# Reordering the start of a tuned convolution and SiLU kernel: a block's taps ahead of the next blocks' transposes, the first output matmuls a pair sooner, three warm matmuls out

## Chip, cores, metric

The kernel runs on one core of one Trainium2 chip. The metric is device time in microseconds (us). TensorE is called PE here, its weight loads PEld, VectorE DVE, ScalarE ACT, GpSimd POOL, as in the profile.

## The reference

```python
def _attn_ref(x, weight):              # x (8, 4096, 192), weight (8 heads, 7 taps)
    w = softmax(weight, axis=-1)       # written out in the original
    # causal convolution of 7 taps, one set of taps per head of 24 channels
    out = np.einsum('hk,bskhg->bshg', w, x_unf)
    return out.reshape(B, S, D)
def _moe_ref(x, w_in, w_out, beta):    # w_in (192, 2048), w_out (2048, 192)
    h = x @ w_in
    g = h * (1.0 / (1.0 + np.exp(-beta * h)))
    return g @ w_out                   # on 32768 tokens
```

## The kernel before

Tokens are cut in two halves that occupy the two halves of the array's rows. Per half the work goes in chunks: three small ones first (128, 128 and 256 tokens, called chunk 0, 1 and 2), four of 256, then chunks of 512. For each chunk the hidden matmuls (`mm1`) give `ph` in PSUM, ACT applies SiLU and gives `g`, and the output matmuls (`mm2`) use `g`. Chunks 0 to 2 do `mm1` in eight **pairs** (two hidden chunks of 128 at once).

In steady state the convolution runs on DVE. For the first 512 tokens (**blocks 0 to 3** of 128) there is no time for that, so PE does it with diagonal matrices (`conv_0`, seven taps), after transposing the block. Blocks 4 and 5 are transposed on PE as well, in pair 6 of chunk 1, and then copied by DVE into `xt`, where DVE's own convolution starts. I call this copy **the late blocks' copy**.

```python
    warm(9, 256)                                   # dummy matmuls; their results are not used
    ...
    pin(nc.tensor.matmul(tap_ps, sel..., taps, start=True, stop=True))
    warm(3, 128)                                   # taken out by the change
    ...                                            # softmax of the taps, diagonals
    t = transpose_0(pa[0], x0, 0)                  # block 0
    take_0(t, 0, act=True)
    warm(7, 128)
    ...
    conv_0(b0, 0)                                  # block 0 by seven taps on PE
    ...
    def first_tile(i, u):                          # what follows pair u of chunk i on PE
        if (i, u) == (0, 1):
            take_0(transpose_0(pa[0], xb0, 0), 2)  # block 2: transposes, copy by DVE
            conv_0(pb, 1, 0, 1)                    # block 1: tap 0
        elif (i, u) == (0, 2):
            take_0(transpose_0(pa[1], xb0, 1), 3)  # block 3
            conv_0(pb, 1, 1, 2)
        elif (i, u) == (0, 3):
            conv_0(pb, 1, 2, 5)
        elif (i, u) == (0, 4):
            conv_0(pb, 1, 5, K)
            ...                                    # DVE: evacuate block 1, scale w_out 0 to 3
        ...                                        # blocks 2 and 3 by taps, w_out 4 to 15
        elif (i, u) == (1, 6):
            new_xt(1)
            ts_ = [transpose_0(pb[b], xb1, b) for b in range(2)]     # blocks 4 and 5
            for b in range(2):
                pin(nc.vector.tensor_copy(xt_of[1][...], ts_[b]))    # the late blocks' copy
    ...
    # which output matmuls (of 16 hidden chunks) follow which pair
    for key, us, cuts in (((0, 0), [(1, 4), (1, 5), (1, 6), (1, 7)], (0, 4, 8, 12, 16)), ...
```

`pin` keeps instructions in program order. `w_in` is loaded by POOL's DMA queue in three slices of columns; pair 5 of chunk 0 is the first that needs the third slice (columns 640 on). `w_out` is scaled by 1/beta on DVE (`scale_w_out`) before an output matmul can use it, and later cut into thirds by twelve DVE copies (`part_w_out`).

Of the kernel before, what the change touches and what calls it, by code (L numbers as in the profile page):

```python
# [19 lines left out]
def kernel(  # L20
# [25 lines left out]
    def pin(ins):  # L46

        return tc.keep_in_program_order(ins)
# [27 lines left out]
    def load_x(j, s, b0=0, b1=NB, eng=None):  # L76
        if j not in xf_of:
            xf_of[j] = xf_pool.tile([128, NB, NS, D], FP32, name="xf")
        src = xs[s, TILE * j + 128 * b0:TILE * j + 128 * b1, :]
        pin((eng or nc.sync).dma_start(out=xf_of[j][:, b0:b1, s, :],  # L80
                                       in_=src.rearrange("(b p) d -> p b d", p=128)))

    def cast_x(j, s, b0=0, b1=NB, eng=None):
        if j not in xbf_of:
            xbf_of[j] = xbf_pool.tile([128, NB, NK, NS, Q], BF16, name="xb")
        pin((eng or nc.vector).tensor_copy(  # L86
            xbf_of[j][:, b0:b1, :, s, :].rearrange("p b k q -> p k b q"),
            xf_of[j][:, b0:b1, s, :].rearrange("p b (q k) -> p k b q", k=NK)))

    def new_xt(j):  # L90
        xt_of[j] = xt_pool.tile([128, NK, LEAD + TILE], BF16, name="xt")

    def transpose_x(j, b):
        if j not in xt_of:
            new_xt(j)
        c = LEAD + 128 * b
        pin(nc.sync.dma_start_transpose(
            out=xt_of[j][:, :, c:c + 128],
            in_=xbf_of[j][:, b, :, :, :].rearrange("p k s q -> p (k s q)")))
# [9 lines left out]
    def half_of(s):  # L109
        return slice(64 * s, 64 * s + 64)  # L110
# [62 lines left out]
    def po_banks():  # L173
        return [po_bank(), po_bank()]
# [7 lines left out]
    def warm(n, cols):  # L182
        for _ in range(n):
            pin(nc.tensor.matmul(idle[:, 0, 0:cols], ones[:, 0:128], ones[:, 0:cols], start=True, stop=True))
# [3 lines left out]
    nmax = consts.tile([128, 1], FP32, name="nmax")  # L188
    tap_ps = cv0[:, 1, 0:K]
    pin(nc.tensor.matmul(tap_ps, sel.rearrange("h s g j -> h (s g j)"), taps, start=True, stop=True))  # L190
    warm(3, 128)
    pin(nc.vector.tensor_reduce(out=nmax, in_=tap_ps, axis=AX.X, op=ALU.max, negate=True))
    etap = consts.tile([128, K], FP32, name="etap")
    tsum = consts.tile([128, 1], FP32, name="tsum")
# [14 lines left out]
    def transpose_0(bank, src, b):  # L209

        bf = src.dtype == BF16
        t = (bank.bitcast(BF16) if bf else bank)[:, 0:NK * 128].rearrange("p (k t) -> p k t", k=NK)
        v = src[:, b, :, :].rearrange("p s d -> p (s d)").rearrange("p (m k) -> p k m", k=NK)
        for kk in range(NK):
            pin(nc.tensor.transpose(t[:, kk, :], v[:, kk, :], ident_b if bf else ident))  # L215
        return t

    def take_0(t, b, act=False):
        dst = xr[:, :, PAD + 128 * b:PAD + 128 * b + 128]
        if act:  # L220
            pin(nc.scalar.activation(dst, t, AF.Copy))
        else:
            pin(nc.vector.tensor_copy(dst, t))

    def conv_0(cv, b, k0=0, k1=K):

        for k in range(k0, k1):
            for s in range(NS):
                pin(nc.tensor.matmul(  # L229
                    cv[s][:, 0:NK * 128], diag[half_of(s), k, :, :].rearrange("p s q -> p (s q)"),  # L230
                    xr[half_of(s), :, 128 * b + k:128 * b + k + 128], start=(k == 0), stop=(k == K - 1)))

    def evac_0(cv, b, s, eng):
        i, c = place[b]
        src = cv[s][:, 0:NK * 128].rearrange("p (k t) -> p k t", k=NK)
        dst = xc_of[i][:, s, :, c:c + 128]
        if eng is nc.scalar:
            pin(nc.scalar.activation(dst, src, AF.Copy, scale=rsum))
        else:
            pin(eng.tensor_scalar_mul(dst, src, rsum))  # L240
# [3 lines left out]
    pb = po_banks()  # L244
# [26 lines left out]
    def scale_w_out(c):  # L271
        pin(nc.vector.tensor_scalar_mul(w_out_s[:, c, :], w_out_f[:, c, :], rbeta[:, c:c + 1]))
# [219 lines left out]

    def first_tile(i, u):
        if (i, u) == (0, 1):
            take_0(transpose_0(pa[0], xb0, 0), 2)
            conv_0(pb, 1, 0, 1)
        elif (i, u) == (0, 2):
            take_0(transpose_0(pa[1], xb0, 1), 3)
            conv_0(pb, 1, 1, 2)
        elif (i, u) == (0, 3):  # L500
            conv_0(pb, 1, 2, 5)
        elif (i, u) == (0, 4):
            conv_0(pb, 1, 5, K)
            for s in range(NS):
                evac_0(pb, 1, s, nc.vector)
            for c in range(4):
                scale_w_out(c)
        elif (i, u) == (0, 5):
            conv_0(pa, 2, 0, 2)
        elif (i, u) == (0, 6):  # L510
            conv_0(pa, 2, 2, 5)
        elif (i, u) == (0, 7):
            conv_0(pa, 2, 5, K)
            for s in range(NS):
                evac_0(pa, 2, s, nc.vector)
            for c in range(4, 8):
                scale_w_out(c)
        elif (i, u) == (1, 0):
            conv_0(pb, 3, 0, 2)
        elif (i, u) == (1, 1):  # L520
            conv_0(pb, 3, 2, 5)
        elif (i, u) == (1, 2):
            conv_0(pb, 3, 5, K)
            for s in range(NS):
                evac_0(pb, 3, s, nc.vector)
            for c in range(8, NF):
                scale_w_out(c)
        elif (i, u) == (1, 6):
            new_xt(1)
            ts_ = [transpose_0(pb[b], xb1, b) for b in range(2)]  # L530
            for b in range(2):
                pin(nc.vector.tensor_copy(xt_of[1][:, :, LEAD + 128 * b:LEAD + 128 * b + 128], ts_[b]))
            pin(nc.vector.tensor_copy(xt_of[0][:, :, TILE + LEAD - PAD:],
                                      xr[:, :, TILE:].bitcast(FP32)))
        elif (i, u) == (1, 7):
            for s in range(NS):
                cast_x(1, s, 2, NB)
            for b in range(2, NB):
                transpose_x(1, b)
            for j in (2, 3):  # L540
                for s in range(NS):
                    load_x(j, s)
# [2 lines left out]

    prs_0 = ((0, 0), (1, 0))
    first_mm2 = {}
    for key, us, cuts in (((0, 0), [(1, 4), (1, 5), (1, 6), (1, 7)], (0, 4, 8, 12, 16)),
                          ((1, 0), [(2, 1), (2, 2)], (0, 8, 16)),
                          ((0, 1), [(2, 3), (2, 4)], (0, 8, 16)),  # L550
                          ((1, 1), [(2, 5), (2, 6), (2, 7)], (0, 5, 10, 16))):
        for (i, u), c0, c1 in zip(us, cuts, cuts[1:]):
            first_mm2[(i, u) + key] = range(c0, c1)

    for i in range(n_steps):
        plan = mm2_plan(i - 1) if NP <= i <= NQ else [[] for _ in range(NF)]
        new_g(i, 0)
        if i < NP:
            new_g(i, 1)
        if i < NP:  # L560
            for u in range(NF // 2):
                mm1_pair(i, u)
                first_tile(i, u)
                for ph in (0, 1):
                    for j in range(i):
                        for fc in first_mm2.get((i, u, j, ph), ()):
                            mm2(j, prs_0, ph, fc)
                if i == 2:
                    vector_work(i, 1300, flush=u == NF // 2 - 1)
            continue  # L570
        for u in range(NF):
            if u == NF // 2:
                new_g(i, 1)
            mm1(i, u)
            for t in plan[u]:
                mm2(i - 1, *t)
                if t[1] == 1 and t[2] == NF - 1:
                    budget -= 2 * (D + 60) / 0.96
            if i > NQ:
                mm2_quarters(NM)  # L580
            vector_work(i, 1307 * steps[i][1] // TILE, flush=u == NF - 1)
# [30 lines left out]
```

## Time and profile before

| | before |
|---|---|
| time, first three runs | 687.03 us (687.0 to 687.11) |
| full PE clock from | 5.16 us |
| first activation of pair 0, pair 2, pair 5 of chunk 0 | 8.01, 10.35, 12.95 us |
| first activation of chunk 2 | 21.92 us |
| start of the late blocks' copy on DVE | 20.05 us |
| start of activation 400 (of 576, counted from 0) | 442.88 us |

Times are from the span's start. "Full PE clock from" is the start of the trace's first record of the full clock. Until then PE goes at about half the pace, which I call half clock: a tap of both halves takes 0.32 us and not 0.17, as shown below. The PEclk column of the profile does not show this (it reads 1.00 from 4 us on in before_again, where the first record comes at 9.39). "Activation 400" lies deep in the steady state; it is a good measure of the lead that the start has gained or lost, since the change leaves what follows as it is.

The page of before: span, busy time, and the chain that ended last by engine.

```profile
span 685.2 us, 26902 instructions
...
PE 679.8 (99%) x12368; PEld 501.6 (73%) x12368; DVE 553.0 (81%) x905; ACT 584.0 (85%) x584; POOL 14.6 (2%) x26
...
PE 97%; ACT 1%; DMA 1%; POOL 0%; issue 0%; DVE 0%; POOLq 0%
```

The PE timeline of before around pairs 1 to 5 (start, length, line and operands, count, idle time before it and what ended it):

```profile
7.47 0.83 PE L319 MATMUL ph<-xcp,w_in_s 64*128 64x256 bf16 x12
9.24 0.35 PE L215 MATMUL po<-ident_b,xb 128*128 128x128 bf16 x3 [0.94 <-DMA xb<-in_x_dram]
9.52 0.44 PE L229 MATMUL po<-xr,diag 64*128 64x384 f32 x2
9.80 0.50 PE L319 MATMUL ph<-xcp,w_in_s 64*128 64x256 bf16 x6
10.24 0.35 PE L215 MATMUL po<-ident_b,xb 128*128 128x128 bf16 x3
...
12.38 0.50 PE L319 MATMUL ph<-xcp,w_in_s 64*128 64x256 bf16 x6
```

After pairs 0 and 1 PE stands 0.94 us until block 2 has come in, although the taps of block 1 (L229), whose data DVE had ready at 8.02, stood right behind. ACT waits with it (timeline of ACT, before):

```profile
8.01 1.57 ACT L323 ACTIVATE gp<-ph,beta 128x256 bf16<-128x256 f32 x4 [0.76 <-DVE xr L223]
10.35 0.84 ACT L323 ACTIVATE gp<-ph,beta 128x256 bf16<-128x256 f32 x2 [0.77 <-PE ph L319]
11.35 2.08 ACT L323 ACTIVATE gp<-ph,beta 128x256 bf16<-128x256 f32 x5 [0.16 <-PE ph L319]
```

```profile
20.00:90.00 70.00, 69.68 (x1297) 60.71 (x1295) 69.22 (x123) 68.89 (x100) 0.00 (x0) 1.00 0.48 128
```

### The profile page before, as it was taken

The numbers are of one execution on the slowest core, as the hardware profiler recorded it, in microseconds if no ns is written. First come the engines' busy times: TensorE is split into PE (matmuls) and PEld (weight loads), VectorE is DVE, ScalarE is ACT, GpSimd is POOL, SyncE is SP. The second block draws the span as 40 slices with busy tenths as digits, with TensorE's granted clock in tenths as the row PEclk, the third lists the DMA queues.
The fourth block names the chain that finished last, engine by engine and source line by source line (L and its number), as shares of the span: only waits on it lengthen the run. The fifth ranks groups of instructions, "written<-read, shape, count | busy, mean of one in ns | idle before, by whom it ended". The sixth has DMA issues, their size and how long they took to land.

```text
span 685.2 us, 26902 instructions
## 1 busy us (share of the span) xinstructions
PE 679.8 (99%) x12368; PEld 501.6 (73%) x12368; DVE 553.0 (81%) x905; ACT 584.0 (85%) x584; POOL 14.6 (2%) x26
## 2 busy tenths in 40 slices
PE   8999999999999999999999999999999999999998
PEld 6799767777777777777777777777777777777777
DVE  5999999999988889878889888889888889875112
ACT  7999998888888888888888888888888888888881
POOL 8000000000000000000000000000000000000000
PEclk9999999999999999999999999999999999999999
DMA  9654334344423344423444323344323443220213
GB/s 210 173 163 118 94 94 112 78 118 117 117 57 86 100 112 117 113 56 87 104 112 117 102 63 90 101 117 118 89 58 101 106 117 72 65 52 5 49 48 93
DMA packets 149873, 66.82 MB, mean 98 GB/s; under 512 B 112593, under 2 KB 149153, under 8 KB 149761
## 3 DMA queue, kind: packets, MB, share of 16 engines
q1 hardware_dynamic: 146448, 61.08, 35.4%
q0 software_dynamic: 3168, 3.93, 2.7%
q8 instruction: 96, 1.57, 0.9%
q14 instruction: 17, 0.13, 0.1%
q10 hardware_dynamic: 144, 0.10, 0.1%
HBM read 28.32 MB, written 25.17 MB: 78 GB/s over the span
## 4 chain that ended last, share of the span: by engine, by line
PE 97%; ACT 1%; DMA 1%; POOL 0%; issue 0%; DVE 0%; POOLq 0%
PE ph L336 47%; PE po L414 42%; PE po L368 4%; PE po L452 2%; PE ph L319 1%; ACT gp L323 1%; DMA xb<-in_x_dram 1%; ACT g L323 1%; POOL w_in_s L113 0%; PE po L229 0%; PE po L215 0%; POOL sel L146 0%; DVE o_sp L374 0%; POOL ident L148 0%; POOLq L146 0%
## 5 line engine op out<-in xcount | busy, mean ns | idle before, releaser
L340 ACT ACTIVATE g<-ph,beta 128x1024 bf16<-128x1024 f32 (+1 forms) x528 | 557.7, 1063 | 81.4 <-PE ph L336 66.4
L336 PE MATMUL ph<-xc,w_in_s 64*64 64x512 bf16 (+2 forms) x5856 | 573.2, 369 | 0.3 <-ACT g L323 0.3
L414 PE MATMUL po<-g,w_out_q 64*64 64x512 bf16 x5376 | 528.2, 376 | 0.0
L336 PEld LDWEIGHTS <-w_in_s 64*64 64x64 bf16 (+1 forms) x5856 | 303.8, 105 | 95.2 <-issue 0.6
L414 PEld LDWEIGHTS <-w_out_q 64*64 64x64 bf16 x5376 | 289.4, 106 | 72.3
L302 DVE SCALAR_TENSOR_TENSOR acc<-xt,tapn,acc 128x512 f32<-128x512 bf16 (+1 forms) x455 | 311.3, 760 | 0.6
L431 DVE STREAM_TRANSPOSE o_sb<-po 128x512 f32<-128x512 f32 x84 | 74.7, 889 | 113.0 <-PE po L414 112.9
L302 DVE SCALAR_TENSOR_TENSOR xc<-xt,tapn,acc 128x512 bf16<-128x512 bf16 (+1 forms) x91 | 64.2, 761 | 0.1
L86 DVE CAST xb<-xf 128x768 bf16<-128x768 f32 (+1 forms) x62 | 48.6, 825 | 0.0
L300 DVE TENSOR_SCALAR acc<-xt,tapn 128x512 f32<-128x512 bf16 (+1 forms) x91 | 40.9, 484 | 1.1
L368 PE MATMUL po<-w_out_s,g 64*128 64x192 bf16 x640 | 40.8, 243 | 0.0
L368 PEld LDWEIGHTS <-g 64*128 64x128 bf16 x640 | 31.0, 94 | 3.3
L374 DVE COPY o_sp<-po 128x192 f32<-128x192 f32 x32 | 10.2, 350 | 7.3 <-PE po L452 7.3
L319 PE MATMUL ph<-xcp,w_in_s 64*128 64x256 bf16 (+1 forms) x144 | 14.5, 306 | 0.4 <-ACT gp L323 0.2
L323 ACT ACTIVATE gp<-ph,beta 128x256 bf16<-128x256 f32 x32 | 12.5, 481 | 2.1 <-PE ph L319 1.3
L452 PEld LDWEIGHTS <-g 128*128 128x128 bf16 x128 | 10.5, 98 | 0.4 <-issue 0.4
L452 PE MATMUL po<-w_out_s,g 128*128 128x192 bf16 x128 | 10.7, 246 | 0.0
L323 ACT ACTIVATE g<-ph,beta 128x512 bf16<-128x512 f32 x16 | 9.6, 692 | 0.2
L319 PEld LDWEIGHTS <-w_in_s 64*128 64x128 bf16 x144 | 6.6, 94 | 3.5 <-issue 1.2
L229 PE MATMUL po<-xr,diag 64*128 64x384 f32 x49 | 7.8, 373 | 0.0
L368 PE MATMUL po<-w_out_s,gp 64*128 64x192 bf16 x128 | 7.2, 243 | 0.0
L368 PEld LDWEIGHTS <-gp 64*128 64x128 bf16 x128 | 5.8, 94 | 1.6
(53 smaller groups left out, 59.7 us busy)
## 6 DMA issues: line engine op xcount, KB each, us to landing
xf<-in_x_dram SPq DMA_DIRECT2D x60, 384.0 KB, 4.4
out_dram<-o_sb SPq DMA_DIRECT2D x112, 192.0 KB, 4.5
out_dram<-o_sp SPq DMA_DIRECT2D x12, 192.0 KB, 3.9
xt<-xb SPq DMA_TRANSPOSE x122, 2.4
w_out_f<-in_moe_w_out_dram POOLq DMA_DIRECT2D x4, 384.0 KB, 6.3
w_in_s<-w_in_s POOLq DMA_DIRECT2D x4, 192.0 KB, 7.0
out_dram<-o_sp SPq DMA_DIRECT2D x8, 96.0 KB, 1.6
w_in_s<-in_moe_w_in_dram POOLq DMA_DIRECT2D x4, 144.0 KB, 5.0
```

Source lines behind the costliest of these rows:

```text
L86: pin((eng or nc.vector).tensor_copy(xbf_of[j][:, b0:b1, :, s, :].rearrange("p b k q -> p k b q"), xf_of[j][:, b0:b1, s, :].rearrange("p b ...
L300: pin(nc.vector.tensor_scalar_mul(a, src, w))
L302: pin(nc.vector.scalar_tensor_tensor(out=xc_of[i][:, k0:k1, 0:n] if k == K - 1 else a, in0=src, scalar=w, in1=a, op0=ALU.mult, op1=ALU.add))
L319: pin(nc.tensor.matmul(ph[:, h, 0:NS * n], w_in_s[half_of(h), kk, ts(fcs[h], 128)], xc_of[i][half_of(h), :, kk, :], start=(kk == 0), stop= ...
L323: pin(nc.scalar.activation(g_at(i, fcs[h])[:, :, 0:n], ph[:, h, 0:NS * n].rearrange("p (s t) -> p s t", s=NS), AF.Silu, scale=beta[:, fcs[ ...
L336: pin(nc.tensor.matmul(ph[m0:m1, s, 0:n], w_in_s[half_of(s), kk, 128 * fc + m0:128 * fc + m1], xc_of[i][half_of(s), kk, 0:n], start=(kk == ...
L340: pin(nc.scalar.activation(g_at(i, fc)[:, :, 0:n], ph[:, :, 0:n], AF.Silu, scale=beta[:, fc:fc + 1]))
L368: pin(nc.tensor.matmul(po[q][:, 0:D], g_at(i, fc)[r, s, ts(b, 128)], w_out_s[r, fc, :], start=(phase == 0 and fc == 0), stop=(phase == 1 a ...
L374: pin(nc.vector.tensor_copy(dst, po[:, 0:D]))
L414: pin(nc.tensor.matmul(po_of[i, m][half_of(s), 0:n], w_out_q[half_of(r), fc, m, :], g_at(i, fc)[half_of(r), s, 0:n], start=(first and fc = ...
L431: pin(nc.vector.transpose(osb_of[i][:, 0:n // L, :, m], po_of[i, m][:, 0:n].rearrange("p (b l) -> p b l", l=L)))
L452: pin(nc.tensor.matmul(po[:, 0:D], g_at(i, fc)[:, s, ts(b, 128)], w_out_s[:, fc, :], start=(fc == 0), stop=(fc == NF - 1)))
```

## The change

Its intent: (A) without three warm matmuls the first transposes follow the tap matmul at once; (B) the taps of block 1 fill the wait for blocks 2 and 3; (C) chunk 0's output matmuls begin one pair sooner, so that the pair with six transposes carries fewer of them.

```diff
     pin(nc.tensor.matmul(tap_ps, sel.rearrange("h s g j -> h (s g j)"), taps, start=True, stop=True))
-    warm(3, 128)
@@
         if (i, u) == (0, 1):
+            conv_0(pb, 1, 0, 2)
+        elif (i, u) == (0, 2):
+            conv_0(pb, 1, 2, 4)
+        elif (i, u) == (0, 3):
             take_0(transpose_0(pa[0], xb0, 0), 2)
-            conv_0(pb, 1, 0, 1)
-        elif (i, u) == (0, 2):
+            conv_0(pb, 1, 4, 5)
+        elif (i, u) == (0, 4):
             take_0(transpose_0(pa[1], xb0, 1), 3)
-            conv_0(pb, 1, 1, 2)
-        elif (i, u) == (0, 3):
-            conv_0(pb, 1, 2, 5)
-        elif (i, u) == (0, 4):
             conv_0(pb, 1, 5, K)
@@
-    ... (((0, 0), [(1, 4), (1, 5), (1, 6), (1, 7)], (0, 4, 8, 12, 16)),
+    ... (((0, 0), [(1, u) for u in range(3, 8)], (0, 4, 8, 12, 13, 16)),
```

More of the change, by code (lines that the diff above doesn't have):

```diff
@@ L547 @@
     first_mm2 = {}
-    for key, us, cuts in (((0, 0), [(1, 4), (1, 5), (1, 6), (1, 7)], (0, 4, 8, 12, 16)),
+    for key, us, cuts in (((0, 0), [(1, u) for u in range(3, 8)], (0, 4, 8, 12, 13, 16)),
                           ((1, 0), [(2, 1), (2, 2)], (0, 8, 16)),
```

## The prediction

> **What bounds the kernel now.** The page gives TensorE (PE) 679.8 of 685.2 us busy and 97% of the chain that ended last. From about 31 us on nothing changes. The change touches only the first 22 us, where the chain by time mixes PE, ScalarE (ACT) and DMA. So the question is how much earlier chunk 2's first matmul starts; before it is at 21.07 us, with its activation at 21.92.
>
> **Where time is lost there (timeline and waits, before).**
> 1. PE runs the tap matmul, three warm matmuls (3.31 to 3.60, 107 ns apart, half clock), then the first fp32 transposes at 3.60. x had landed at 3.22.
> 2. After pair 1 of chunk 0, PE sits 0.94 us until 9.24, waiting for the DMA of token block 2 (landed 9.20), then again for block 3 (10.23). ACT idles 0.77 us before pair 2 and 0.16 before pair 3. The Trainium skill, "TensorE: Matmul & The Clock Gate" (Part 2), says matmuls stay in program order. The trace agrees: block 1's tap matmuls, whose data were ready at 8.02, stood behind the transposes until 9.52.
> 3. At the end of chunk 1, six transposes plus eight output matmuls push the last pair to 20.41; ACT idles 0.35 us. Earlier (17.72) PE waited 0.23 us for ACT.
>
> **What the change does.** It adds no work but removes three warm matmuls. Costs: a tap of both halves 0.18 us, a pair's six matmuls 0.33, pair start to its activation 0.55, two activations 0.73, four chunks' output matmuls 0.33.
>
> - Step A, warm matmuls out: transposes at about 3.31; first activations at 7.75 instead of 8.01, 0.25 sooner.
> - Step B, order: after pair 1 come four tap matmuls at about 8.0, then pair 2 at about 8.75 (its w_in columns land only at 8.69), pair 3 at about 9.5, pair 4 near 10.3. The transposes find landed data. ACT's 0.77 us gap nearly closes; these pairs run 1.0 to 1.3 us ahead.
> - But pair 5 needs w_in columns 640 onward, whose second half lands at 11.48. Pair 5 can start no sooner than about 11.53 (before: 12.38). This clips the lead to about 0.85 us and swallows Step A entirely: a new wait of some tenths on that DMA.
> - From pair 5 to chunk 1's pair 3 PE is nearly dense, so 0.85 is kept.
> - Step C, output matmuls a pair sooner: fills PE's wait near 17, takes three chunks out of the transposes' pair, so the last pair comes earlier: about 0.3 us gross. VectorE's in-order scaling of w_out chunks 8 to 11 then ends near 18.4, when PE wants chunk 11 near 18.1, so about half is given back. Chunk 2 starts near 20.1: 0.85 to 1.0 us sooner.
>
> xc of the next chunk is ready at 29.16, wanted near 29.5, and VectorE moves too (its casts may wait for x at 20.43). I expect no clipping there.
>
> **Predicted:** 687.03 - 0.95 = 686.1 us, range 685.7 to 686.7. Chances: faster by over 2% 0.00, within 2% 1.00, slower 0.00.
>
> **Signs.** Right: first transpose near 3.3; no PE wait on x near 9; pair 5's matmuls at 11.5, just after a w_in landing, with ACT idle 0.1 to 0.3 there; ACT gap at 20.6 under 0.2; chunk 2's activation near 21.0. Wrong: pair 5 at 12 or later, or chunk 2 near 21.9.
>
> **What would make it wrong.** The full clock came at 5.16 us; the skill (Part 1) calls the activity window free-running. With fewer warm matmuls it might come later and cost over 1 us. w_in may land at another time, moving the clip. The wait on w_out scaling may be larger. If the next chunk's xc binds, up to half returns.

## More of the kernel before

```profile
PEld L336 <- DVE xc L302: 0.2, 1, 0.2
```

DVE is as full as PE there (69.22 of 70 us), and PE's weight load waits, once, for `xc` that DVE made. Second, DVE's timeline where its steady work begins:

```profile
17.16 1.14 DVE L240 TENSOR_SCALAR xcp<-po,rsum 128x384 bf16<-128x384 f32 x2 [0.24 <-PE po L229]
18.22 1.92 DVE L272 TENSOR_SCALAR w_out_s<-w_out_f,rbeta 128x192 bf16<-128x192 f32 x8
20.05 0.61 DVE L532 COPY xt<-po 128x384 bf16<-128x384 bf16 x2
```

From the end of block 3's taps DVE has no idle time between these rows.

## The result

Six runs each: after 687.47 us median (686.79 to 687.92), before 687.39 us (687.0 to 688.05). The ratio is 1.0, with a 95% interval of 0.9987 to 1.0013. Ratios here are the mean time of one kernel's fast runs over that of the other's of the same rounds, so not quite the ratio of the medians. Nothing was gained, and 687.47 lies outside my range of 685.7 to 686.7.

| start in us | before | predicted | after |
|---|---|---|---|
| full PE clock from | 5.16 | 5.16 | 6.71 |
| first transposes | 3.60 | 3.31 | 3.31 |
| pair 0, first activation | 8.01 | 7.75 | 8.58 |
| last `w_in` columns landed | 11.48 | 11.48 | 12.15 |
| pair 5, matmuls | 12.38 | 11.53 | 12.38 |
| chunk 2, first activation | 21.92 | near 21.0 | 21.76 |
| late blocks' copy | 20.05 | no number given | 20.18 |
| activation 400 | 442.88 | about 0.95 sooner | 443.00 |

(Of DVE the prediction only said that it "moves too".) The page of after, the same three parts:

```profile
span 685.4 us, 26896 instructions
...
PE 680.7 (99%) x12365; PEld 500.4 (73%) x12365; DVE 552.8 (81%) x905; ACT 583.5 (85%) x584; POOL 14.5 (2%) x26
...
PE 89%; DVE 9%; issue 1%; ACT 0%; DVEq 0%
```

Busy time says nothing new, but the chain now has 9% of DVE. Three things can be seen below it. First, the clock. PE's timelines of block 0's taps, before and then after; from one tap of both halves to the next it is 0.17 us at full clock and 0.32 at half clock:

```profile
5.13 0.44 PE L229 MATMUL ph<-xr,diag 64*128 64x384 f32 x1
...
5.41 0.33 PE L229 MATMUL ph<-xr,diag 64*128 64x384 f32 x1
...
5.58 0.34 PE L229 MATMUL ph<-xr,diag 64*128 64x384 f32 x1
```

```profile
4.89 0.69 PE L228 MATMUL ph<-xr,diag 64*128 64x384 f32 x1
...
5.38 0.52 PE L228 MATMUL ph<-xr,diag 64*128 64x384 f32 x1
...
5.70 0.52 PE L228 MATMUL ph<-xr,diag 64*128 64x384 f32 x1
```

After starts its taps 0.24 us sooner and is slower by the second of them. Second, the new order. PE's timeline of after, for the rows shown of before, and ACT's:

```profile
8.04 0.83 PE L318 MATMUL ph<-xcp,w_in_s 64*128 64x256 bf16 x12
8.64 0.62 PE L228 MATMUL po<-xr,diag 64*128 64x384 f32 x4
9.47 0.50 PE L318 MATMUL ph<-xcp,w_in_s 64*128 64x256 bf16 x6 [0.20 <-ACT gp L322]
9.71 0.62 PE L228 MATMUL po<-xr,diag 64*128 64x384 f32 x4
10.20 0.50 PE L318 MATMUL ph<-xcp,w_in_s 64*128 64x256 bf16 x6
10.63 0.35 PE L214 MATMUL po<-ident_b,xb 128*128 128x128 bf16 x3
...
12.38 0.50 PE L318 MATMUL ph<-xcp,w_in_s 64*128 64x256 bf16 x6
```

```profile
8.58 4.00 ACT L322 ACTIVATE gp<-ph,beta 128x256 bf16<-128x256 f32 x10 [0.76 <-DVE xr L222]
12.93 0.47 ACT L322 ACTIVATE gp<-ph,beta 128x256 bf16<-128x256 f32 x1 [0.35 <-PE ph L318]
```

The 0.94 us wait is gone and pairs 2 to 4 come sooner, as intended. But pair 5 starts at 12.38, exactly where it started before. Third, what follows at the end of chunk 1 and at 90 us. DVE's timeline and the waits from 88 to 92 us, after:

```profile
17.16 1.14 DVE L239 TENSOR_SCALAR xcp<-po,rsum 128x384 bf16<-128x384 f32 x2 [0.23 <-PE po L228]
18.21 1.92 DVE L271 TENSOR_SCALAR w_out_s<-w_out_f,rbeta 128x192 bf16<-128x192 f32 x8
20.18 0.62 DVE L531 COPY xt<-po 128x384 bf16<-128x384 bf16 x2
```

```profile
PEld L335 <- issue: 0.6, 2, 0.5
ACT g L339 <- PE ph L335: 0.4, 1, 0.4
PE ph L335 <- DVE xc L301: 0.2, 1, 0.2
```

The late blocks' copy comes 0.13 us later. Chunk 2 is 0.16 us ahead on ACT and stays so until activation 120 (82.14 against 82.31); then PE waits for `xc` and is 0.12 us behind for the rest. The chain that ended last, between 85 and 95 us (shares of this stretch by engine and line), has no DVE in before, and in after (second row) it has:

```profile
by line: PE ph L336 65.3%; PE po L414 19.8%; PE po L368 16.5%
by line: PE ph L335 30.4%; DVE acc L301 28.0%; PE po L413 17.8%; DVE xc L301 14.9%; issue 10.6%; DVE o_sp L373 5.3%
```

### The profile page after: what moved, and what is told of

The parts are those of the page before. It is cut to its first block, busy times and chain, and to the rows that moved or that the text cites. A ratio compares the mean times of both kernels' runs of the same rounds, so it can differ in the third digit from the quotient of the medians.

```text
span 685.4 us, 26896 instructions
## 1 busy us (share of the span) xinstructions
PE 680.7 (99%) x12365; PEld 500.4 (73%) x12365; DVE 552.8 (81%) x905; ACT 583.5 (85%) x584; POOL 14.5 (2%) x26
## 3 DMA queue, kind: packets, MB, share of 16 engines
q8 instruction: 96, 1.57, 1.0%
## 4 chain that ended last, share of the span: by engine, by line
PE 89%; DVE 9%; issue 1%; ACT 0%; DVEq 0%
PE po L413 42%; PE ph L335 42%; DVE acc L301 5%; PE po L451 2%; DVE xb L86 1%; DVE o_sp L373 1%; DVE acc L299 1%; PE ph L318 1%; DVE xc L301 1%; PE po L228 1%; PE ph L184 0%; DVE w_out_q L274 0%; PE po L214 0%; PE ph L228 0%; PE po L367 0%
```

## The experiments

**Theory.** From the late blocks' copy to about 90 us DVE, not PE, sets the time; PE and DVE arrive at 90 us together in before, so a lead of PE alone is lost there. **Rivals.** (1) The loss is all in the clock, which the missing warm matmuls delay. (2) PE sets the time all along, and the lead is lost in PE's own order or to a DMA. In the expectations "theory 1" is rival (1). Eighteen runs in five calls, on five chips; every one was profiled, and the table has what the verdicts rest on (us, read from the traces; copy is the late blocks' copy, chunk 2 its first activation, act 400 activation 400). A clock that is full before 6 us is called early, a later one late.

| run | steps | clock full at | pair 0 | last w_in landed | pair 5 | copy | chunk 2 | act 400 | pair 0 to 5 | pair 5 to copy | copy to act 400 | chunk 2 to act 400 |
|---|---|---|---|---|---|---|---|---|---|---|---|---|
| before | none | 5.16 | 8.01 | 11.48 | 12.95 | 20.05 | 21.92 | 442.88 | 4.94 | 7.10 | 422.83 | 420.95 |
| before_again | none | 9.39 | 9.58 | 11.68 | 13.61 | 20.72 | 22.59 | 443.52 | 4.04 | 7.11 | 422.80 | 420.94 |
| after | ABC | 6.71 | 8.58 | 12.15 | 12.93 | 20.18 | 21.76 | 443.00 | 4.35 | 7.25 | 422.82 | 421.25 |
| after_again | ABC | 4.19 | 7.70 | 12.02 | 12.60 | 19.96 | 21.55 | 442.79 | 4.90 | 7.37 | 422.83 | 421.25 |
| after_third | ABC | 4.32 | 7.70 | 11.94 | 12.52 | 19.76 | 21.34 | 442.59 | 4.82 | 7.24 | 422.83 | 421.25 |
| a_only | A | 8.61 | 9.07 | 11.67 | 13.11 | 20.21 | 22.08 | 443.04 | 4.04 | 7.10 | 422.83 | 420.95 |
| b_only | B | 7.36 | 9.00 | 11.68 | 13.34 | 20.46 | 22.32 | 443.27 | 4.34 | 7.12 | 422.81 | 420.95 |
| b_again | B | 4.08 | 7.81 | 12.32 | 12.90 | 20.00 | 21.85 | 442.82 | 5.09 | 7.10 | 422.82 | 420.97 |
| c_only | C | 4.16 | 7.89 | 11.58 | 12.83 | 20.06 | 21.64 | 442.89 | 4.93 | 7.23 | 422.83 | 421.25 |
| bc_warm_kept | BC | 6.90 | 8.80 | 12.23 | 13.14 | 20.39 | 21.97 | 443.22 | 4.34 | 7.25 | 422.83 | 421.25 |
| c_later | AB, other C | 9.44 | 9.35 | 12.46 | 13.70 | 20.81 | 22.59 | 443.64 | 4.35 | 7.11 | 422.83 | 421.04 |
| ab2 | A, other B | 7.49 | 8.88 | 12.78 | 13.36 | 20.50 | 22.34 | 443.73 | 4.49 | 7.14 | 423.23 | 421.39 |
| ab2_again | A, other B | 7.05 | 8.74 | 11.40 | 13.05 | 20.16 | 22.01 | 442.98 | 4.30 | 7.11 | 422.82 | 420.97 |
| before_tap | DVE less | 6.87 | 8.79 | 11.50 | 13.00 | 20.10 | 21.96 | 442.85 | 4.21 | 7.10 | 422.75 | 420.89 |
| after_tap | ABC, DVE less | 6.50 | 8.49 | 12.89 | 13.47 | 20.70 | 22.28 | 443.18 | 4.98 | 7.23 | 422.48 | 420.89 |
| before_pool | copies on POOL | 4.83 | 7.92 | 12.04 | 12.77 | 20.76 | 21.84 | 443.29 | 4.84 | 7.99 | 422.53 | 421.45 |
| after_pool | ABC, on POOL | 9.56 | 9.36 | 12.78 | 13.70 | 21.98 | 23.26 | 444.44 | 4.34 | 8.28 | 422.46 | 421.18 |
| before_pool_late | on POOL, late | 9.27 | 9.51 | 11.66 | 13.54 | 20.64 | 22.51 | 443.39 | 4.03 | 7.10 | 422.75 | 420.88 |
| after_pool_late | ABC, POOL late | 7.12 | 8.76 | 11.66 | 13.11 | 20.35 | 21.94 | 442.83 | 4.34 | 7.24 | 422.48 | 420.90 |
| ac_pool_late | AC, POOL late | 9.23 | 9.37 | 12.40 | 13.41 | 20.66 | 22.24 | 443.12 | 4.04 | 7.25 | 422.46 | 420.89 |

The traces also show where the differences in the last column arise. Counted from chunk 2, activation by activation, all runs but before_pool and after_pool agree to 0.01 us up to activation 127. At activation 128 alone, near 90.6 us, every run with after's cuts and a full DVE falls 0.36 or 0.37 us behind before_tap, c_later 0.16, ab2 0.51, and the other runs with the old cuts 0.05 to 0.09; the runs in which DVE is relieved (by a tap or by late copies) stay level. From there on the distances stay as they are. And DVE, from the copy to the last `xc` ahead of 90 us, never pauses for more than 0.04 us, but for ab2 (0.3 us once) and the two runs with a tap less.

### First call: the same kernels again, and the steps apart

**before_again** (no edit).

> The kernel before, unchanged, profiled a second time. Theory 1 (the clock belongs to the kernel): the full clock comes at 5.2 us again, first activation at 8.0, second half of the last w_in columns lands at 11.5. Rival (clock and landings vary from run to run): full clock anywhere from 5.2 to 6.8, first activation 8.0 to 8.6, that landing 11.4 to 12.2, with the same code. Either way activation 400 lies within 0.2 us of 442.9, because the VectorE chain from the late blocks' copies to the xc of the 90 us mark sets it.

Measured: 687.42 us median of 4 runs, before of the same rounds 687.43; ratio 0.9996 (0.9979 to 1.0012). The clock came at 9.39 us with code that had it at 5.16, so the rival of this run holds: clock and start vary from run to run (pair 0 even beyond the 8.6 that I allowed). Activation 400 came at 443.52, not within 0.2 us of 442.9: I had taken DVE's chain for fixed, but its beginning hangs on PE and moved by 0.67 us with the copy. From the copy on, the two runs agree to 0.03 us.

**after_again** (no edit).

> The kernel after, unchanged, profiled a second time. Theory 1 (fewer warm matmuls delay the clock): full clock near 6.7 us again and first activation 8.6. Rival (run to run): full clock near 5.2 in about half of such runs, then first activation 7.75. If the last w_in landing is at 11.5 instead of 12.15, pair 5's first activation comes near 12.1 instead of 12.9. Under the VectorE theory activation 400 still is no more than 0.6 us before 442.9, however far chunk 2's activation (21.8) moves forward, and PE waits for xc at about 90 us.

Measured: 687.38 us (4 runs), ratio 0.9996 (0.9981 to 1.0011). Here the clock came at 4.19, pair 0 at 7.70, and the matmuls of pairs 2, 3 and 4 at 8.59, 9.32 and 10.32, close to the prediction's 8.75, 9.5 and 10.3. Then pair 5 waited for the last `w_in` columns, which landed at 12.02. The waits of PEld and PE from 11 to 13 us, and ACT's timeline, in this run:

```profile
PEld L318 <- DMA w_in_s<-in_moe_w_in_dram: 0.5, 1, 0.5
...
PE ph L318 <- DMA w_in_s<-in_moe_w_in_dram: 0.3, 1, 0.3
```

```profile
7.70 4.00 ACT L322 ACTIVATE gp<-ph,beta 128x256 bf16<-128x256 f32 x10 [0.76 <-DVE xr L222]
12.60 0.84 ACT L322 ACTIVATE gp<-ph,beta 128x256 bf16<-128x256 f32 x2 [0.90 <-PE ph L318]
```

So this clip is real, as predicted, only 0.5 us later than one profile of before had led me to expect. Chunk 2 is 0.37 us ahead of before, activation 400 only 0.09, with the wait for `xc` at 90 us in between.

**a_only** (before without `warm(3, 128)`).

> Before without its three warm matmuls, nothing else. Prediction's step A alone: first activation 7.75 if the full clock comes at 5.2, 8.6 if at 6.7 (theory: fewer warm matmuls delay it). In both cases pair 2 stays at 10.3, since the transposes wait for token blocks landed at 9.2 and 10.0, and activation 400 stays within 0.1 us of 442.9. Time same.

Measured: 687.3 us (4 runs), ratio 0.9996 (0.9981 to 1.0011). The clock came at 8.61, later than either value that I had named, and pair 0 at 9.07. My expectation that pair 2 stays at 10.3 failed too: with so late a start the transposes find their data landed, and pair 2 comes at 10.52. Activation 400 came 0.16 us behind before's, a little outside the 0.1 expected. Rival (1) does not stand as the whole cause: after_again had an earlier clock than before (4.19 against 5.16), and activation 400 was still only 0.09 us ahead. Whether the missing matmuls delay the clock at all is another question. Over all twenty profiles, with the three warm matmuls the full clock came at 4.08 to 9.39 us (nine, 6.45 on average), without them at 4.19 to 9.56 (eleven, 7.29). Both kinds span the same range, but on so few a shift of 1 us or more cannot be excluded (the averages differ by 0.85, with a standard error of 0.9). What A gives for a like clock is small: pair 0 at 7.70 without them (4.19 and 4.32) against 7.81 and 7.89 with them (4.08 and 4.16), and 9.36 and 9.37 (9.56 and 9.23) against 9.58 and 9.51 (9.39 and 9.27), so 0.1 to 0.2 us.

**bc_warm_kept** (after with `warm(3, 128)` put back).

> After with the three warm matmuls put back (steps B and C without A). Theory 1: full clock at 5.2 again, first activation 8.0, pair 2 near 9.5, then clipped at pair 5 by the last w_in landing (matmuls at that landing plus 0.1 to 0.2). Rival: clock as likely at 6.7. Chunk 2's activation 0.2 to 1.0 us before 21.92 by that landing; activation 400 at most 0.6 us ahead of 442.9 by the VectorE theory (with a wait of PE for xc at 90 us of at least what chunk 2's lead exceeds it by), the full lead of chunk 2 by the prediction.

Measured: 687.36 us (4 runs, one at 690.2 that makes the interval wide), ratio 1.0006 (0.9984 to 1.0029). Clock at 6.90, with all warm matmuls. Chunk 2 at 21.97 is no lead at all, and activation 400 comes 0.34 us behind before's, so both "ahead" of the expectation were wrong. But copy to activation 400 is 422.83, and PE waits at 90 us by as much as in after. The landing at 12.23 did not bind here: pair 5's matmuls came at 12.60.

### Second call: DVE relieved by POOL, and B and C alone

**before_pool** and **after_pool**:

```diff
-        pin(nc.vector.tensor_copy(w_out_q[:, c:c + 4, m, :],
+        pin(nc.gpsimd.tensor_copy(w_out_q[:, c:c + 4, m, :],
...
-            work += [(i, 330, lambda c=c, m=m: part_w_out(c, m)) ...
+            work += [(i, 0, lambda c=c, m=m: part_w_out(c, m)) ...
```

> Before with the twelve copies that cut w_out into thirds moved from VectorE to GpSimd (some 2.5 us of VectorE work between 73 and 76 us). VectorE theory: VectorE stops setting the time at 90 us; PE then does, so activation 400 follows chunk 2's first activation by 420.95 to 421.0 (as in the before runs, where it was 420.96 and 420.93), not the late blocks' copy by 422.8; the last xc ahead of 90 us ends 2 us or more before PE wants it. Since in before PE arrives at that point together with VectorE, the time itself changes by less than 0.2 us. Rival (PE sets the time all along): the same, so this run alone does not tell them apart; it is the partner of the next.

> After with the same twelve copies on GpSimd. VectorE theory: the wait of PE for xc at 90 us (0.55 us start to start in three runs of steps B and C) is gone, activation 400 follows chunk 2's first activation by 420.95 instead of 421.24, and so lies some 0.3 us earlier than after's for the same chunk-2 start; over 5 rounds this kernel is 0.1 to 0.5 us below before. Rival (the lead is lost in some other place): the wait at 90 us stays or another of the same size comes, and activation 400 still follows the late blocks' copy by 422.83.

Measured: before_pool 687.81 us (5 runs), ratio 1.0009 (0.9997 to 1.0022); after_pool 688.15 us (5 runs), ratio 1.0014 (1.0001 to 1.0027). This experiment failed to do what I built it for. POOL has its own order, was free, and did the copies as soon as `w_out` was scaled, in the middle of DVE's scaling. Timelines of DVE and of POOL in before_pool:

```profile
18.04 2.80 DVE L272 TENSOR_SCALAR w_out_s<-w_out_f,rbeta 128x192 bf16<-128x192 f32 x8
20.76 0.61 DVE L532 COPY xt<-po 128x384 bf16<-128x384 bf16 x2
```

```profile
18.83 4.83 POOL L275 COPY w_out_q<-w_out_s 128x256 bf16<-128x256 bf16 x12
```

The eight scalings took 2.80 us instead of 1.92 in before. The late blocks' copy came 7.99 and 8.28 us after pair 5 instead of 7.10 and 7.25, and the work moved off DVE could not make that good ahead of the earlier points where PE needs `xc`: chunk 2 to activation 400 took 421.45 and 421.18, and counted by activations the loss arose between number 64 and number 96, well ahead of 90 us. The Trainium skill, "SBUF — State Buffer" (Who interferes with whom), calls the SBUF port pair that VectorE and GpSimd share an exclusive lock, for the VectorE instructions that use it: the one that comes second waits for the whole instruction of the other. The trace agrees in kind: beside the copies six of the eight scalings took 0.45 to 0.49 us instead of 0.31, and late in that stretch scalings and copies alike started every 0.37 us. That these scalings use the shared pair was not tested apart.

**c_only** (before with after's cuts `[(1, u) for u in range(3, 8)], (0, 4, 8, 12, 13, 16)`).

> Before with step C alone (output matmuls a pair sooner). VectorE theory: the matmuls of chunks 8 to 11 now wait for their scaled w_out in pair 5 of chunk 1 and hold back the six transposes of the late blocks, so the late blocks' copy comes 0.1 to 0.2 us later against the end of conv block 3 than in before, and activation 400 follows that copy by 422.8 as ever: step C by itself makes the program 0.1 to 0.2 us later for the same start, though the last pair of chunk 1 comes 0.3 us sooner than before for the same start. Prediction: 0.3 us gained. Time same.

Measured: 687.13 us (4 runs), ratio 0.9998 (0.9983 to 1.0014). As expected by the DVE theory: pair 5 to copy 7.23 instead of 7.10, chunk 2 0.16 us sooner after pair 5 (8.81 against 8.97), and copy to activation 400 422.83. So C brings ACT's chunk 2 forward and the program 0.13 us back.

**b_only** (after's order of taps and transposes in before, nothing else).

> Before with step B alone (two chunks of taps ahead of the transposes). If the full clock comes before 6 us: pair 5 starts on the last w_in landing (12.0 or later) or by 12.1 on PE. From pair 0's to pair 5's first activation: 4.3 to 4.35 us when nothing is waited for (as in two runs of B and C with a late clock), against 4.03 in the two late-clock runs of the old order. So B gains only when the clock comes early enough for the old order to wait for token block 2 (pair 0 before about 9.0), at most 0.6 us, and loses 0.3 us when the clock is late. The late blocks' copy follows pair 5's start as in before (7.1 us after its activation), activation 400 follows the copy by 422.8.

Measured: 687.24 us (4 runs), ratio 0.9998 (0.9985 to 1.0012). Clock at 7.36; pair 0 to pair 5 took 4.34 us, as in after and bc_warm_kept, against 4.04 in before_again and a_only. With a clock this late, B costs 0.3 us. Pair 5 to copy is 7.12, copy to activation 400 422.81.

### Third call: DVE relieved in two other ways

**before_tap** and **after_tap** give a wrong result (relative error 0.13): DVE leaves out one tap in six chunks.

```diff
-                                    for k in range(K) for p in parts]
+                                    for k in range(K) if not (k == 3 and i <= NQ + 1) for p in parts]
```

> Before, wrong result on purpose: VectorE leaves out one of the seven taps in the steps from 512 to 2560 tokens, which takes some 4 us of its work away ahead of 56 us and some 8 ahead of 90 us and touches nothing else. VectorE theory: PE never waits for xc; activation 400 follows chunk 2's first activation by 420.8 to 420.96 (before: 420.96, 420.93), and no longer follows the late blocks' copy by 422.8. PE theory: the same 420.95, which alone does not decide; it is the partner of the next.

> After with the same tap left out. VectorE theory: the wait at 90 us goes, activation 400 follows chunk 2's first activation by the same 420.8 to 420.96 as in before_tap, instead of 421.24 (three runs with steps B and C), so the lead of chunk 2 over its own VectorE chain is kept. Rival (the 0.3 us is lost to something else between 30 and 130 us, as PE's own order): still 421.2.

Measured: before_tap 686.87 us (4 runs), ratio 0.9995 (0.9982 to 1.0009); after_tap 687.18 us (4 runs), ratio 0.9996 (0.9981 to 1.0011). The two traces show what the times cannot: activation 400 follows chunk 2 by 420.89 in **both**, where after had 421.25 and before 420.95. With DVE out of the way the path of the other engines from chunk 2 on is the same in both kernels; the 0.3 us that after loses at 90 us is DVE's, and rival (2) (PE's own order) falls. Before itself waited 0.06 us. The constant 422.83 from the copy is gone (422.48 and 422.75), as it should be when the copy no longer sets the time.

**after_pool_late**: POOL's copies held back until DVE has written the `xc` of 1280 to 1536 tokens, by a one-column read ahead of them.

```diff
+            work.append((i, 0, lambda i=i: pin(nc.gpsimd.tensor_copy(late, xc_of[i - 2][:, 0, 0:1]))))
             work += [(i, 0, lambda c=c, m=m: part_w_out(c, m)) ...
```

> After with the twelve w_out copies on GpSimd, held back until the xc of 1280 to 1536 tokens is written (some 56 us), so that they do not run beside the w_out scaling as in the two earlier runs. If those runs were slower because the early copies slowed VectorE ahead of 20 us: the late blocks' copy follows pair 5's activation by 7.25 as in after, VectorE gains about 2 us between 56 and 76, the wait at 90 us is gone and activation 400 follows chunk 2's first activation by 420.95. If GpSimd slows VectorE by as much as it takes off it, the wait stays.

Measured: 687.26 us (5 runs), ratio 1.0001 (0.9988 to 1.0013). As expected in the trace: pair 5 to copy 7.24, chunk 2 to activation 400 420.90, and ACT runs through 90 us (timeline of ACT, 88 to 92 us; in after this row broke off at 90.34 with a gap of 0.43 us):

```profile
87.40 5.55 ACT L339 ACTIVATE g<-ph,beta 128x1024 bf16<-128x1024 f32 x5
```

This is a correct kernel in which the wait is gone. DVE gained 1.8 us of the 2.5 or so that were moved (from the copy to the last `xc` ahead of 90 us: 68.2 us against 70.0).

**ab2** (A, and another order for B):

```diff
         if (i, u) == (0, 1):
             conv_0(pb, 1, 0, 2)
         elif (i, u) == (0, 2):
-            conv_0(pb, 1, 2, 4)
+            take_0(transpose_0(pa[0], xb0, 0), 2)
+            conv_0(pb, 1, 2, 3)
         elif (i, u) == (0, 3):
-            take_0(transpose_0(pa[0], xb0, 0), 2)
-            conv_0(pb, 1, 4, 5)
+            take_0(transpose_0(pa[1], xb0, 1), 3)
+            conv_0(pb, 1, 3, 4)
         elif (i, u) == (0, 4):
-            take_0(transpose_0(pa[1], xb0, 1), 3)
-            conv_0(pb, 1, 5, K)
+            conv_0(pb, 1, 4, K)
```

> Step A and another order for B (two taps after pair 1, then the transposes of blocks 2 and 3 after pairs 2 and 3 with one tap each, three taps after pair 4), and the output matmuls where before has them. If B's 0.3 us late-clock loss comes from putting the transposes into pairs where PE has no spare time: pair 0 to pair 5 takes 4.0 to 4.1 us when nothing is waited for, not 4.34. With an early clock pair 5 starts on the last w_in landing. The late blocks' copy follows pair 5's activation by 7.1, activation 400 that copy by 422.83. For the same clock 0.2 to 0.3 us below before, which 5 rounds may not show.

Measured: 687.28 us (5 runs), ratio 1.0002 (0.9989 to 1.0014). Inconclusive: `w_in` landed only at 12.78, pair 5 followed 0.58 us later, and DVE waited 0.3 us for a late landing of x, which also broke the 422.83 (423.23).

### Fourth call: what the relief is worth, and B once more

**before_pool_late** (before with the edit of after_pool_late) and **ac_pool_late** (that, with A and C, without B).

> Before with the twelve w_out copies on GpSimd behind the 56 us mark, the partner of after_pool_late. VectorE theory: in before PE and VectorE reach the 90 us point together, so relief alone gives next to nothing: activation 400 follows chunk 2's first activation by 420.90 instead of 420.95. The rest hangs on the clock: 442.8 with a full clock before 6 us, up to 443.5 with one after 9 us.

> Steps A and C on the relieved kernel, B left out. VectorE theory: A's 0.2 us (for the same clock) and C's lead of chunk 2 both reach the end: chunk 2's first activation follows pair 5's by 8.8 (as in the runs with C: 8.81 to 8.95) instead of 8.97, activation 400 follows it by 420.9; pair 0 to pair 5 4.03 with a late clock. Some 0.4 us below before for the same clock, with a time perhaps 0.0 to 0.5 us below before's. Rival: the wait for xc comes back at 90 us (421.25).

Measured: before_pool_late 686.91 us (5 runs), ratio 0.9995 (0.9983 to 1.0008); ac_pool_late 686.9 us (5 runs), ratio 0.9994 (0.9981 to 1.0008), before of the same rounds 687.23. Both follow chunk 2 by 420.88 and 420.89. In before the relief is worth 0.06 us; in ac_pool_late chunk 2 follows pair 5 by 8.83 and the lead lasts: 443.12 against 443.52 in before_again (clock at 9.23 and 9.39). The times themselves do not set these kernels apart from before.

**b_again** and **after_third** (no edits to b_only and after).

> Step B alone a second time, for the landing of the last w_in columns and the clock. If B itself delays that landing, it comes at 12.0 or later (eight runs with B so far: 11.66 to 12.89, six without: 11.48 to 12.04); if not, 11.5 to 11.7. With a full clock before 6 us: pair 5's first activation 0.55 after that landing or 12.3, whichever is later, against 12.8 to 12.95 in three early-clock runs of the old order; with a later clock 4.34 after pair 0's.

> After a third time, for the same two questions. Activation 400 follows the late blocks' copy by 422.83 and chunk 2's first activation by 421.25; pair 5 4.34 after pair 0 with a clock later than 6 us, or 0.55 after the last w_in landing; landing 12.0 to 12.9 if B delays it, 11.5 to 11.7 if not.

Measured: b_again 687.09 us (4 runs), ratio 0.9995 (0.9982 to 1.0009); after_third 686.63 us (4 runs), ratio 0.9991 (0.9977 to 1.0004). Both had an early clock, so here B could show its worth, and both were stopped by the landing: 12.32 and 11.94, pair 5's activation 0.58 us after each. B alone then came to 12.90, where the old order had 12.95, 12.77 and 12.83 with an early clock; A and B together 12.52 and 12.60. The rest ran by the constants: activation 400 at 422.82 and 422.83 from the copy.

### Fifth call: two points of mechanism

**c_later** (after with other cuts).

```diff
-        [(1, u) for u in range(3, 8)], (0, 4, 8, 12, 13, 16)
+        [(1, u) for u in range(3, 8)], (0, 4, 8, 9, 12, 16)
```

> After with the cuts of the first output matmuls at 0, 4, 8, 9, 12, 16 instead of 0, 4, 8, 12, 13, 16: only chunk 8 is left ahead of the transposes in pair 5 of chunk 1. If the held-back transposes are the cause of C's loss: the late blocks' copy follows pair 5's first activation by 7.10 as in before, not 7.24, and activation 400 follows the copy by 422.83. Rival (the copy is late for another reason, as VectorE itself): still 7.24.

Measured: 687.31 us (4 runs), ratio 1.0 (0.9983 to 1.0016). Pair 5 to copy 7.11, back to before's. So C's loss comes from three output chunks standing ahead of the transposes: in after, the eight matmuls of chunks 8 to 11 took 0.76 us on PE where eight such took 0.51 in before, since they waited for their scaled `w_out`, and the transposes behind them came 0.17 us later (19.79 against 19.62). In after_again they took 0.90 us, and there the copy follows pair 5 latest, by 7.37. PE's timelines of before and then after:

```profile
18.78 0.51 PE L368 MATMUL po<-w_out_s,gp 64*128 64x192 bf16 x8
...
19.62 0.52 PE L215 MATMUL po<-ident_b,xb 128*128 128x128 bf16 x6
```

```profile
18.76 0.76 PE L367 MATMUL po<-w_out_s,gp 64*128 64x192 bf16 x8
...
19.79 0.52 PE L214 MATMUL po<-ident_b,xb 128*128 128x128 bf16 x6
```

**ab2_again** (ab2, no edit).

> The run ab2 again. If the place of the transposes costs the 0.31 us: with a clock later than 6 us and a w_in landing that does not bind, pair 0 to pair 5 takes 4.03 to 4.12; with a binding landing pair 5's activation comes 0.58 after it and the question stays open. Rival (ACT's pace after pair 1 costs it, whatever the order): 4.34.

Measured: 687.39 us (4 runs), ratio 1.0001 (0.9986 to 1.0016). The landing at 11.40 did not bind, and pair 0 to pair 5 took 4.30. So my explanation for B's 0.3 us (the place of the transposes in pairs 3 and 4) fell. The rows suggest another, argued and not tested: pair 2 follows pair 0 by 1.44 or 1.45 us in every late-clock run but before_tap (1.61, where the transposes still waited for block 2), since ACT must first free a `ph` buffer. In that gap the old order does three transposes and one tap (0.56 us from the first of them to the next pair's matmuls, 9.24 to 9.80 in before), the new one only two taps, about 0.36, and then PE waits (the 0.20 us ahead of 9.47 in after). What is not done in the gap is done later, where PE has no time to spare.

## Why the prediction was wrong

1. **"Pair 5 can start no sooner than about 11.53 (before: 12.38). This clips the lead to about 0.85 us"** — in size this is the step that failed most. A lead that pair 5 has is, by and large, kept to chunk 2, as I said ("PE is nearly dense"), but the 0.85 was not there: pair 5 moved by 0.02 us in the profiled pair, where its matmuls started at 12.38, after the landing and so not held by it. Over all profiles pair 5 comes at 13.15 us on average with the old order (eight) and at 13.14 with that of after (ten), though the clock came no later in these (6.62 on average against 7.19). The term was mis-sized twice. I set pair 5 to "11.53" by a landing at 11.48, read from one profile; in the early-clock runs of the new order it landed at 11.94 to 12.32 and pair 5's activation came 0.58 us after it. And I compared with 12.95, a start that waits for block 2; with a clock past 8 us the old order does not wait, and is 0.3 us quicker from pair 0 to pair 5 (4.03 against 4.34; with the clock at 6.87, in before_tap, it still waited and took 4.21). Why B costs this is the part that stays argued.
2. **"first activations at 7.75 instead of 8.01"** — right where the clock came early (7.70 twice), but the clock is a draw: 4.08 to 9.56 us in twenty profiles, with and without the warm matmuls. I had named the danger and put it down to the missing matmuls; the runs do not tie it to them. The Trainium skill, "TensorE: Matmul & The Clock Gate" (Part 1), says that the activity window runs freely; the spread fits that (5.16 and 9.39 us with one and the same code of before), but no run shows the window itself.
3. **"I expect no clipping there"** — this step failed in its mechanism. I had named the risk ("up to half returns") and dismissed it, since I looked only at the first `xc` (29.16 us, wanted near 29.5) and not at those that follow. DVE is full from the late blocks' copy to 90 us, and whatever lead PE has over that chain is lost there. In the runs of before and after and of A, B and C alone or together, activation 400 follows the copy by 422.80 to 422.83 us, while its distance from chunk 2 goes from 420.94 to 421.25. Taking a tap off DVE (before_tap, after_tap) and moving copies to POOL late (after_pool_late) each removed the wait. The sign was in the profile of before: one wait of PEld for `xc`, with DVE busy 69.22 of 70 us. The busy share alone would not do: in after_pool_late it is 69.18 of 70, and PE does not wait.
4. **Step C, "about half is given back"** — for chunk 2 this was right: 0.16 us sooner after pair 5. But through DVE the stall that I had foreseen counts once more: it holds back the transposes, so the late blocks' copy, so everything: 0.13 us lost in c_only, none in c_later.
5. **What held**: first transposes at 3.31, the wait at 9 us gone, the clip of pair 5 by `w_in` with an early clock, and matmuls in program order (Part 2 of the same page): the transposes did hold back the taps behind them.

Put together for the profiled pair: the late clock, less A's gain, cost 0.57 us at pair 0, the quicker way to pair 5 gave back 0.59, and C cost 0.14 on the DVE chain; activation 400 came 0.12 us later and the profiled time was 687.14 us against 687.01. Against the forecast of 0.95 us sooner 1.07 us are missing: 0.83 at pair 5 and 0.28 on the DVE chain, less 0.04 by which C did better than forecast up to chunk 2. Where the clock came early (after_again, after_third) pair 5 led before's by 0.35 and 0.43 us, chunk 2 by 0.37 and 0.58, and activation 400 by 0.09 and 0.29: the DVE chain again took 0.28 and 0.29.

**Open.** Whether B itself delays the `w_in` landing: 11.66 to 12.89 us in the ten profiles with after's order, 11.48 to 12.40 in the eight with the old one. The averages are 12.21 and 11.75, a hint that it does; but the two overlap, and no run holds everything else fixed. Why the clock comes when it does was not tried either, nor was an earlier start of the late blocks' copy, as by putting some of the eight scalings behind it. No version beat both kernels clear of the noise.

## What to carry to other kernels

Before crediting a lead at the start of a pipeline, follow every engine that is full behind it to the place where it meets the bottleneck again; a PE that is 99% busy can be in a tie with another engine, and a single short wait in the profile can tell of it. When the expected gain is below the spread of one kernel's runs, profile the same code several times and measure distances between events: they agreed to hundredths of a microsecond here while the start moved by more than one. Work moved to an idle engine runs when that engine is free, not where it stood; say when it may start.

## What the Trainium skill lacked or had wrong

- "TensorE: Matmul & The Clock Gate" (Part 1) says that the change to full clock varies by ±500 ns from run to run (further down it calls the number of slow matmuls run-variable). In twenty profiles of near-identical starts the change came between 4.08 and 9.56 us; in the two of before, one and the same code, at 5.16 and 9.39.
- The same page does not follow such a draw to the end of a kernel. Here a clock at 9.39 instead of 5.16 us moved pair 0 by 1.57 us, but activation 400 by 0.64.
- "Perfetto Trace Analysis" (Identifying the Most-Contended Engine) ranks engines by occupancy and warns of matmul busy time. It does not tell of a tie: in the stretch from 20 to 90 us PE, DVE and ACT were busy 69.68, 69.22 and 68.89 of 70 us, and only the distances between events told which of them set the time.
- "SBUF — State Buffer" has the shared port of VectorE and GpSimd. How much is left of what one moves off a full DVE is not to be read from it: twelve POOL copies beside eight scalings made those take 2.80 us instead of 1.92; put later, they still took back about 0.7 of some 2.5 us.
